# Register loads between the halves of the second product, other scatter slots, other unit periods

## The chip, the core and the metric

The kernel runs on one core of a Trainium2 chip. The metric is the device time of one execution in microseconds; the time of a kernel is the median of its runs. TensorE (PE) multiplies matrices, VectorE (DVE) and ScalarE (ACT) work elementwise, GpSimd (POOL) does elementwise work and issues indirect DMAs, SyncE (SP) issues the other DMAs. Every engine executes its own instructions in program order and waits for the others by semaphores.

## What is computed

A gated linear recurrence over four sequences of 5056 tokens with 256 features, and behind it a mixture of eight experts, of which each token goes to one:

```python
f = lower_bound + (1 - lower_bound) * sigmoid(f_logit)
h = f[:, t] * h + (1 - f[:, t]) * x[:, t]      # for t in range(S); y[:, t] = h
...
logits = y @ w_gate                            # 20224 tokens x 8 experts
e = argmax(logits); gate_w = softmax(logits)[e]
out = gate_w * (relu(y @ w1[e]) @ w2[e])       # w1: 256 x 1024, w2: 1024 x 256
```

## The kernel before

**Front part.** Tokens come in 79 units of 256 (UNIT), with the features on the partitions. For each unit: load (L253), gates on ScalarE and GpSimd (`prep`, L260), the recurrence as a scan on VectorE and the largest magnitude of the result (`scan`, L270), a split into two 16-bit parts (`split`, L290, whose first instruction is the TensorE broadcast L115), and the eight-column router product (`logits`, L315, matmuls L319). After a group of two or four units `route` (L322) picks the expert of each token, and `place` (L343, matmuls L351) counts, for every token, its row in a bucket of its expert. A scatter (L379) then copies 128 token rows into the buckets in HBM: one cast of the row numbers on DVE (L381) and one indirect DMA on POOL (L382). `tile_info` (L397) names the tiles of 128 or 256 tokens that are certain to be full by then; a function `give` (L620) puts them on the list `todo`.

**Expert part.** `fetch` (L500) reads a tile back transposed (SP, L506), with factor and target row (L508), up to three steps ahead. `gemm1` (L513) first loads, for each tile of the step, the offset of its expert's weights into a TensorE register (L515), then makes the first product in four blocks (L526 to L528, three matmuls for the 16-bit parts); a block goes from PSUM through ScalarE (L531) and DVE (L532) into hT. `gemm2` (L552) makes the second product for two halves of 128 tokens, 24 matmuls each (L560 to L562), scales the result (L566) and scatters it to the output by an indirect DMA on POOL (L567). A step takes either two tiles of 128 tokens, in general of two experts, or one of 256. The plan makes all tiles of the first 14 groups 128 tokens long, and those of the later groups 256; a rest of 128-token tiles comes at the end. `step` (L685) runs gemm1 of a new step and then gemm2 of the step before.

**Addresses.** Weight operands have addresses of the form register plus constant. `share_addresses` (L828) rewrites TensorE's stream: it collects up to 16 such sums in a block of register instructions ahead of the matmuls that use them, and starts a new block when 16 are exceeded or a register load comes.

**The order.** After a start written out by hand (ORDER, L44), up to unit 8 and the first step, the loop at L799 interleaves the two parts, in program order, on PE, ACT and DVE. A step has eight slots, and each calls `fill(k)` (L784): k = 0 to 3 after the four blocks of gemm1, 4 in the middle of the first half of gemm2, 5 between the halves, 6 in the middle of the second half, 7 at the end. A unit is planned by `plan_unit` (L776) at a slot number `nxt`: split there, the scan of the next unit two slots later, the gates of the one after it at three, logits at five, the end of a group at ten; `nxt` then moves on by a period of 5 to 8 slots, the longer the more tokens are ready (`ready()`, L673: tokens in `todo` and fetched). Scatters and the `give` behind them wait in the list `held`, and `release` (L628) takes pieces off it: one in slots 0, 2 and 4, one in slots 1 and 3 when more than 6 are held, and two in every slot when fewer than SHORT tokens are ready.

Of the kernel before, what the change touches and what calls it, by code (L numbers as in the profile page):

```python
# [19 lines left out]
E = 8  # L20
F = 1024
NF = F // P
UNIT = 256
GRU = 4
G = 2 * GRU
WE = 2 * 2 * F
# [7 lines left out]
HOWS = ('dve', 'dve', 'dve', 'dve', 'dve', 'dve', 'dve', 'dve', 'dve', 'dve', 'dve', 'dve', 'dve', 'pe', 'pool', 'dve')  # L34
PLO = '000000000011'
DRIP = 1
BACKLOG = 6
MAYBE = 3
LEAD2 = UNIT
LOW = 4 * UNIT  # L40
MID = 5 * UNIT
HIGH = 8 * UNIT
SHORT = 3 * UNIT
ORDER = "Q L X P X T Z L X L A0 P L X X L A1 W T B0 P X L L L P C0 T B1 T F P X Q A2 C1 Q P L A3 B2 L B3 C2 C3 L X T X T L L L F Z X L A4 B4 A6 T P P A5 X T C4 L P B5 B6 C5 C6 F A7 B7 T S Q C7"  # L44
EXPM = 0x7F800000
EVEN = 0x7F000000
# [13 lines left out]
def guaranteed(n, size):  # L60

    return max(0, (n - E * (size - 1)) // size)
# [3 lines left out]
def moe_kernel(ctx: ExitStack, tc: tile.TileContext, x, fl, lb, wg, w1, w2, cst, tok, out, xb, S):  # L66
    nc = tc.nc
# [157 lines left out]
    vals = [(const.tile([P, 3, E], F32, tag=f"val{k}", name=f"val{k}"), {}) for k in range(2)]  # L225
    unit_of, counts = [1], {}
    tk = const.tile([P, NT], I32, tag="tk", name="tk")
    scatters = []

    def free(d, *groups, keep=()):  # L230

        for k in groups:
            tc.declare_no_dep(d.ins, group=k, keep=[s.ins for s in keep], reason="different rows")
# [266 lines left out]
    def fetch(t, tiles):  # L500
        xT = p2.tile([P, 4, UNIT], F16, tag="xT", name=f"xT{t}", bufs=3)
        me = sm.tile([P, 2, 2], F32, tag="me", name=f"me{t}", bufs=5)
        n = 0
        for nt, (off_ap, _, _, skip, nsc) in tiles:
            off = nc.sync.value_load(off_ap, min_val=0, max_val=E * CAP + P - nt)
            d = nc.sync.dma_start_transpose(xT[:, :, n:n + nt], xb16[ds(off, nt), 0:2 * D])  # L506
            guard(d, nsc, skip)
            d = nc.sync.dma_start(me[:, n // P:(n + nt) // P, :], xb[ds(off, nt), D:D + 2].rearrange("(j p) w -> p j w", p=P))  # L508
            guard(d, nsc, skip)
            n += nt  # L510
        return t, tiles, xT, me, n

    def gemm1(t, tiles, xT, me, n, fill):  # L513
        hT = p2.tile([P, 2, NF, UNIT], F16, tag="hT", name=f"hT{t}")
        evs = [nc.tensor.value_load(i[1], min_val=0, max_val=(E - 1) * WE) for _, i in tiles]  # L515
        for b in range(NF // 2):
            ps = pg1.tile([P, 2, UNIT], F32, tag="g1", name=f"g1_{t}_{b}")
            for q in range(2):
                f = 2 * b + q
                a = 0  # L520
                for ev, (nt, _) in zip(evs, tiles):
                    for c in range(2):
                        hi = w1s[:, ds(ev + (c * F + f * P), P)]
                        lo = w1s[:, ds(ev + (2 * F + c * F + f * P), P)]
                        o = ps[:, q, a:a + nt]
                        nc.tensor.matmul(o, lhsT=hi, rhs=xT[:, c, a:a + nt], start=c == 0, stop=False)  # L526
                        nc.tensor.matmul(o, lhsT=hi, rhs=xT[:, 2 + c, a:a + nt], start=False, stop=False)  # L527
                        nc.tensor.matmul(o, lhsT=lo, rhs=xT[:, c, a:a + nt], start=False, stop=c == 1)  # L528
                    a += nt
            hh = hT[:, 0, 2 * b:2 * b + 2, :n]  # L530
            nc.scalar.activation(hh, ps[:, :, :n], AF.Relu)  # L531
            nc.vector.scalar_tensor_tensor(hT[:, 1, 2 * b:2 * b + 2, :n], ps[:, :, :n], 0.0, hh, op0=ALU.max, op1=ALU.subtract)  # L532
            drip(DRIP)
            fill(b)
        return t, n, [ev for ev, (nt, _) in zip(evs, tiles) for _ in range(nt // P)], hT, me, tiles

    def factors(t, n, evs, hT, me, tiles):
        fac = sm.tile([P, 2], F32, tag="fac", name=f"fac{t}", bufs=3)
        ti, a = [], 0
        for nt, (_, _, ei, skip, _) in tiles:  # L540
            j = slice(a // P, (a + nt) // P)
            nc.scalar.activation(fac[:, j], me[:, j, 0], AF.Copy, scale=ei)
            to = me.bitcast(I32)[:, j, 1:2]
            if skip is not None:
                at = sm.tile([P, 1], I32, tag="ti", name=f"ti{t}_{a}", bufs=4)
                nc.vector.tensor_scalar(at, to[:, 0, :], skip, None, op0=ALU.add)
                to = at.unsqueeze(1)
            ti += [to[:, k, :] for k in range(nt // P)]
            a += nt
        return t, evs, hT, fac, ti  # L550

    def gemm2(t, evs, hT, fac, ti, fill):  # L552
        for j, ev in enumerate(evs):
            po = pg2.tile([P, 512], F32, tag="g2", name=f"g2_{t}_{j}")
            for f in range(NF):
                hi = w2s[:, ds(ev + f * D, D)]
                lo = w2s[:, ds(ev + (2 * F + f * D), D)]
                hh = hT[:, 0, f, j * P:(j + 1) * P]
                hl = hT[:, 1, f, j * P:(j + 1) * P]
                nc.tensor.matmul(po[:, :D], lhsT=hh, rhs=hi, start=f == 0, stop=False)  # L560
                nc.tensor.matmul(po[:, :D], lhsT=hh, rhs=lo, start=False, stop=False)  # L561
                nc.tensor.matmul(po[:, :D], lhsT=hl, rhs=hi, start=False, stop=f == NF - 1)  # L562
                if f == NF // 2 - 1:
                    fill(4 + 2 * j)
            ob = p2.tile([P, D], F32, tag="ob", name=f"ob{t}_{j}", bufs=3)
            nc.scalar.activation(ob, po[:, :D], AF.Copy, scale=fac[:, j:j + 1])  # L566
            d = nc.gpsimd.indirect_dma_start(  # L567
                out=out[:, :], out_offset=bass.IndirectOffsetOnAxis(ap=ti[j], axis=0),
                in_=ob, in_offset=None, bounds_check=N - 1, oob_is_err=False)
            free(d, "out")  # L570
            tc.add_to_no_dep_group("out", d.ins)
            fill(5 + 2 * j)
# [3 lines left out]
    while n < NU:  # L576
# [3 lines left out]
        k = guaranteed(n * UNIT - taken, size)  # L580
# [13 lines left out]
    todo, placing, drips, total, held = [], [], [], [], []  # L594
# [33 lines left out]
    def release(n=1):  # L628

        while n and held:  # L630
            held.pop(0)()
            n -= 1

    def drip(n=1):

        for _ in range(n):
            if drips and next(drips[0], True):
                drips.pop(0)
# [32 lines left out]
    queue, fetched, pend, nst = [], [], [], 0  # L671

    def ready():  # L673
        return sum(t for t, _ in todo) + sum(f[4] for f in fetched)

    def prefetch():
        nonlocal nst
        while todo and len(fetched) < 3:
            tiles = [todo.pop(0)]
            if tiles[0][0] == P and todo and todo[0][0] == P:  # L680
                tiles.append(todo.pop(0))
            fetched.append(fetch(nst, tiles))
            nst += 1

    def step(fill, second=True):  # L685

        prefetch()
        if len(pend) > 1:
            gemm2(*factors(*pend.pop(0)), lambda k: None)
        last = factors(*pend.pop(0)) if pend and second else None  # L690
        pend.append(gemm1(*fetched.pop(0), fill))
        prefetch()
        if last:
            gemm2(*last, fill)
        else:
            for k in range(4, 8):
                fill(k)
# [33 lines left out]
    for w in ORDER.split():  # L731
        k, n = w[0], int(w[1:] or 0)
# [43 lines left out]
    def plan_unit(t1, period):  # L776

        nonlocal nxt
        scans1, preps2, split1, logits1 = t1
        coming.extend((nxt + k, a) for k, a in ((0, split1), (2, scans1), (3, preps2), (5, logits1), (10, finish)))  # L780
        coming.sort(key=lambda c: c[0])
        nxt += period

    def fill(k):  # L784
        nonlocal here
        while coming and coming[0][0] <= here:
            coming.pop(0)[1]()
        here += 1
        short = ready() < SHORT
        if short or k in (0, 2, 4) or k in (1, 3) and len(held) > BACKLOG:  # L790
            release(1 + short)

    def flush():
# [5 lines left out]
    while u < NU or coming:  # L799
        r = ready()  # L800
        while u < NU and nxt < here + 8:
            nxt = max(nxt, here)
            plan_unit(tick(u), 5 if r < LOW else 6 if r < MID else 7 if r < HIGH else 8)
            u += 1
        if r >= LEAD2:
            step(fill)
        else:
            flush()
# [6 lines left out]
    while todo or fetched:  # L815
        step(lambda k: None)
# [3 lines left out]
    if spare:  # L820
        n = nc.values_load(total[0])
        last = [fetch(nst + k, tiles) for k, tiles in enumerate((spare[:1], spare[1:]))]
        with tc.If(n > NTAIL - MAYBE):
            for f in last:
                gemm2(*factors(*gemm1(*f, lambda k: None)), lambda k: None)
# [89 lines left out]
```

## Time and profile before

| | |
|---|---|
| median of 3 runs | 1103.1 us (1101.06 to 1103.48) |
| the profiled execution | 1098.53 us, span 1096.8 us |
| mean granted TensorE clock | 0.947 |
| HBM | 58.57 MB read, 43.16 MB written |
| scatters into the buckets, L382 | 158, of 1009 ns each on POOL |
| scatters to the output, L567 | 142 and 20, of 1051 and 971 ns |

In a line of the profile, an engine's busy time is the time in which it has an instruction of its own in work; matmuls overlap, so the 273 ns that one takes at L560 are not the distance between two of them. An idle time in brackets in the timeline is the gap in front of that instruction, with what ended it; "issue" there means that nothing the profile shows was waited for. Register instructions have no rows.

### The profile page before, as it was taken

How to read it: one execution, taken by the hardware profiler on the slowest of the kernel's cores; microseconds unless marked ns; L12 is line 12 of the kernel's file. 1: busy time of each engine (PE TensorE's matmuls, PEld its weight loads, DVE VectorE, ACT ScalarE, POOL GpSimd, SP SyncE). 2: the span in 40 equal slices, each digit the busy share in tenths (PEclk: the TensorE clock that was granted, in tenths of full speed). 3: DMA queues.
4: the chain of work that ended last, by engine and by line, in shares of the span. 5: the costliest groups of instructions: out<-in, count | busy, mean ns of one | idle time of the engine just before them, and what ended most of it. 6: DMA issues, size and time to landing. Idle time of an engine off the chain costs nothing.

```text
span 1096.8 us, 29865 instructions
## 1 busy us (share of the span) xinstructions
PE 956.6 (87%) x10971; PEld 861.8 (79%) x10971; DVE 660.6 (60%) x1827; ACT 497.3 (45%) x971; POOL 509.2 (46%) x517
## 2 busy tenths in 40 slices
PE   3327878988998899998899999999998999999995
PEld 2326777878887788897888888888887888899994
DVE  5789867777656667566677877766655222222321
ACT  4537544545444444454455555545532333333331
POOL 2453765455555455656566665565544112121121
PEclk9557999889999999999999999999999999999998
DMA  7987565776785557656576786677642222222120
GB/s 255 314 274 211 113 134 140 156 145 135 142 157 136 125 133 160 150 137 153 135 177 142 168 175 155 157 142 156 134 104 79 49 50 54 51 53 48 37 49 23
DMA packets 239776, 145.57 MB, mean 133 GB/s; under 512 B 205965, under 2 KB 207247, under 8 KB 237584
## 3 DMA queue, kind: packets, MB, share of 16 engines
q1 hardware_dynamic: 224272, 102.02, 43.8%
q0 software_dynamic: 15360, 41.60, 12.5%
q8 instruction: 93, 1.52, 0.6%
q14 instruction: 51, 0.42, 0.1%
HBM read 58.57 MB, written 43.16 MB: 93 GB/s over the span
## 4 chain that ended last, share of the span: by engine, by line
PE 68%; DVE 14%; issue 8%; ACT 3%; DMA 2%; another core or an unknown queue 2%; POOL 1%; SPq 0%; POOLq 0%; DVEq 0%; ACTq 0%
PE g L528 11%; PE g L526 11%; PE g L527 11%; PE g L560 11%; PE g L562 11%; PE g L561 11%; DVE xt L283 3%; DVE hT L532 2%; DMA ft<-in_f 2%; DVE ft L310 2%; DVE am L286 1%; ACT ft L301 1%; ACT hT L531 1%; PE tp L319 1%
## 5 line engine op out<-in xcount | busy, mean ns | idle before, releaser
L526 PE MATMUL g<-xT,w1s 128*128 128x128 f16 (+1 forms) x1968 | 414.8, 241 | 30.5 <-issue 16.8
L527 PE MATMUL g<-xT,w1s 128*128 128x128 f16 (+1 forms) x1968 | 414.4, 240 | 8.8 <-issue 8.6
L528 PE MATMUL g<-xT,w1s 128*128 128x128 f16 (+1 forms) x1968 | 414.3, 240 | 8.4 <-issue 8.3
L532 DVE SCALAR_TENSOR_TENSOR hT<-g,hT 128x512 f16<-128x512 f32 x324 | 220.2, 687 | 297.1 <-ACT hT L531 256.0
L561 PE MATMUL g<-w2s,hT 128*128 x1296 | 354.2, 273 | 2.6 <-issue 2.6
L560 PE MATMUL g<-w2s,hT 128*128 x1296 | 354.2, 273 | 2.3 <-issue 1.9
L562 PE MATMUL g<-w2s,hT 128*128 x1296 | 354.1, 273 | 0.9 <-issue 0.7
L531 ACT ACTIVATE hT<-g 128x512 f16<-128x512 f32 x324 | 185.6, 591 | 196.0 <-PE g L528 144.2
L382 POOL DMA_INDIRECT buckets<-rows,idx x158 | 159.5, 1009 | 184.7 <-DVE idx L381 120.9
L567 POOL DMA_INDIRECT out_dram<-ob,me x142 | 149.3, 1051 | 194.1 <-ACT ob L566 143.2
L526 PEld LDWEIGHTS <-w1s 128*128 x1968 | 197.1, 100 | 38.0 <-issue 30.0
L527 PEld LDWEIGHTS <-w1s 128*128 x1968 | 197.3, 100 | 24.6 <-issue 17.5
L528 PEld LDWEIGHTS <-w1s 128*128 x1968 | 197.5, 100 | 19.3 <-issue 12.3
L566 ACT ACTIVATE ob<-g,fac 128x256 f32<-128x256 f32 x162 | 76.0, 470 | 179.0 <-PE g L562 161.9
L560 PEld LDWEIGHTS <-hT 128*128 128x128 f16 x1296 | 127.0, 98 | 19.2 <-issue 5.2
L562 PEld LDWEIGHTS <-hT 128*128 128x128 f16 x1296 | 127.1, 98 | 17.8 <-issue 2.8
L561 PEld LDWEIGHTS <-hT 128*128 128x128 f16 x1296 | 127.0, 98 | 15.7 <-issue 1.9
L283 DVE TENSOR_TENSOR_SCAN xt<-ft,xt,xt 128x256 f32<-128x256 f32 (+2 forms) x156 | 113.8, 754 | 5.9 <-POOL xt L268 5.9
L310 DVE SCALAR_TENSOR_TENSOR ft<-xt,m,ft 128x256 f16<-128x256 f32 x154 | 81.2, 546 | 58.2 <-ACT ft L301 44.5
L301 ACT ACTIVATE ft<-xt,m 128x512 f16<-128x512 f32 x79 | 57.0, 721 | 119.1 <-DVE m L298 83.0
L268 POOL TENSOR_TENSOR xt<-gi,xt 128x512 f32<-128x512 f32 x79 | 104.0, 1316 | 5.5
L267 POOL TENSOR_SCALAR gi<-ft 128x512 f32<-128x512 f32 x79 | 57.1, 722 | 78.1 <-ACT ft L265 74.5
(134 smaller groups left out, 755.9 us busy)
## 6 DMA issues: line engine op xcount, KB each, us to landing
ft<-in_f SPq DMA_DIRECT2D x79, 256.0 KB
xt<-in_x SPq DMA_DIRECT2D x79, 256.0 KB
w2s<-in_w SPq DMA_DIRECT2D x14, 1024.0 KB
rows<-ft SPq DMA_TRANSPOSE x158
buckets<-rows,idx POOLq DMA_INDIRECT x158
out_dram<-ob,me POOLq DMA_INDIRECT x142
ws<-in_w SPq DMA_DIRECT2D x2, 1024.0 KB
xT<-buckets SPq DMA_TRANSPOSE x126
```

Of the source, the lines that this page charges most:

```text
L268: nc.gpsimd.tensor_tensor(xt, gi, xt, op=ALU.mult)
L283: nc.vector.tensor_tensor_scan(xt[:, c, a:b], ft[:, c, a:b], xt[:, c, a:b], ini, op0=ALU.mult, op1=ALU.subtract)
L382: d = nc.gpsimd.indirect_dma_start(out=xb[:, :], out_offset=bass.IndirectOffsetOnAxis(ap=idx[:, i:i + 1], axis=0), in_=rows[:, i, 0:ROW], ...
L526: nc.tensor.matmul(o, lhsT=hi, rhs=xT[:, c, a:a + nt], start=c == 0, stop=False)
L527: nc.tensor.matmul(o, lhsT=hi, rhs=xT[:, 2 + c, a:a + nt], start=False, stop=False)
L528: nc.tensor.matmul(o, lhsT=lo, rhs=xT[:, c, a:a + nt], start=False, stop=c == 1)
L531: nc.scalar.activation(hh, ps[:, :, :n], AF.Relu)
L532: nc.vector.scalar_tensor_tensor(hT[:, 1, 2 * b:2 * b + 2, :n], ps[:, :, :n], 0.0, hh, op0=ALU.max, op1=ALU.subtract)
L560: nc.tensor.matmul(po[:, :D], lhsT=hh, rhs=hi, start=f == 0, stop=False)
L561: nc.tensor.matmul(po[:, :D], lhsT=hh, rhs=lo, start=False, stop=False)
L562: nc.tensor.matmul(po[:, :D], lhsT=hl, rhs=hi, start=False, stop=f == NF - 1)
L567: d = nc.gpsimd.indirect_dma_start(out=out[:, :], out_offset=bass.IndirectOffsetOnAxis(ap=ti[j], axis=0), in_=ob, in_offset=None, bounds_c ...
```

## The change

Four constants and the condition for `release` change; the register loads move into a function `bases`, which remembers what it has loaded; and `step` hands gemm2 a `then` that calls `bases` for the next step's tiles in slot 5, before that slot's other work. If no tiles are fetched by then, or the step has no gemm2, gemm1 loads the registers itself as before.

```diff
-BACKLOG = 6
-LOW = 4 * UNIT
+LOW = 3 * UNIT
 MID = 5 * UNIT
-HIGH = 8 * UNIT
-SHORT = 3 * UNIT
+HIGH = 7 * UNIT
+SHORT = 2 * UNIT
...
-    scatters = []
+    scatters, based = [], {}
...
+    def bases(t, tiles):
+
+        if t not in based:
+            based[t] = [nc.tensor.value_load(i[1], min_val=0, max_val=(E - 1) * WE) for _, i in tiles]
+        return based[t]
+
     def gemm1(t, tiles, xT, me, n, fill):
         hT = p2.tile([P, 2, NF, UNIT], F16, tag="hT", name=f"hT{t}")
-        evs = [nc.tensor.value_load(i[1], min_val=0, max_val=(E - 1) * WE) for _, i in tiles]
+        evs = bases(t, tiles)
...
         prefetch()
+
+        def then(k):
+            if k == 5 and fetched:
+                bases(*fetched[0][:2])
+            fill(k)
         if last:
-            gemm2(*last, fill)
+            gemm2(*last, then)
...
         short = ready() < SHORT
-        if short or k in (0, 2, 4) or k in (1, 3) and len(held) > BACKLOG:
+        if short or k in (1, 3) or k == 0 and len(held) > 4 or k == 5 and len(held) > 8:
             release(1 + short)
```

A step with more than LOW, MID and HIGH tokens ready plans its units at periods of 6, 7 and 8 slots, below LOW at 5.

## The prediction

> **What bounds the kernel now.** I read the engines' busy times first, then the stretches, then who TensorE waited for, then single places in the timeline.
>
> ```profile
> span 1096.8 us, 29865 instructions
> PE 956.6 (87%) x10971; PEld 861.8 (79%) x10971; DVE 660.6 (60%) x1827; ACT 497.3 (45%) x971; POOL 509.2 (46%) x517
> ...
> 104.00:300.00 196.00, 167.92 (x2184) 154.92 (x2183) 143.90 (x459) 96.19 (x197) 112.70 (x116) 0.92 0.66 137
> 300.00:560.00 260.00, 233.60 (x3080) 211.38 (x3078) 171.68 (x473) 127.65 (x266) 144.09 (x145) 0.99 0.64 145
> 560.00:800.00 240.00, 233.87 (x2339) 208.47 (x2337) 172.73 (x481) 128.37 (x258) 145.18 (x148) 1.00 0.70 154
> 800.00:850.00 50.00, 45.31 (x405) 38.23 (x403) 27.17 (x111) 14.40 (x31) 21.90 (x22) 0.97 0.37 91
> 850.00:1050.00 200.00, 200.00 (x2198) 183.56 (x2196) 54.26 (x91) 68.15 (x140) 36.91 (x38) 1.00 0.23 50
> ```
>
> The columns of a stretch are its length, then busy time (and instructions) of PE, PEld, DVE, ACT, POOL, then granted clock, DMA share and GB/s. The reader is to see that TensorE is the bound wherever expert products run: from 850 us on it has no gap at all, and no change to planning can shorten that part. What can be won lies in its gaps: 28.1 us in 104 to 300, 26.4 in 300 to 560 (steps of two 128-token tiles up to here), 6.1 in 560 to 800 (steps of one 256-token tile), 4.7 in 800 to 850. The first 104 us, before the planned loop, are not touched. The clock adds to it: a mean grant of 0.92 over 196 us, if it switches between full and half, is 16% or 31 us at half, so about 16 us of work lost, and another 3 us in the next stretch; those are estimates from this column.
>
> ```profile
> PE g L526 <- issue: 16.2, 20, 2.1
> PE g L528 <- issue: 7.4, 15, 1.1
> PE g L527 <- issue: 7.4, 16, 1.0
> PE tp L115 <- DVE am L286: 5.5, 3, 2.1
> PE g L526 <- DVE hT L532: 4.1, 3, 3.2
> PE tp L115 <- DVE idx L381: 4.0, 3, 2.4
> PE g L526 <- DMA xT<-buckets: 2.5, 1, 2.5
> ```
>
> These are TensorE's waits between 104 and 560 us: total, times, longest. The largest releaser is "issue", which means that no semaphore held the instruction: TensorE's own instruction stream was late. Where the long ones sit shows in the timeline:
>
> ```profile
> 143.49 0.23 PE L526 MATMUL g<-xT,w1s 128*128 128x128 f16 x1 [1.87 <-issue]
> ...
> 232.11 0.23 PE L115 MATMUL tp<-half,am 128*128 128x128 bf16 x1 [2.38 <-DVE idx L381]
> 234.41 0.28 PE L526 MATMUL g<-xT,w1s 128*128 128x128 f16 x1 [2.07 <-issue]
> ...
> 261.41 0.23 PE L526 MATMUL g<-xT,w1s 128*128 128x128 f16 x1 [0.39 <-PE tp L319]
> ...
> 274.48 0.23 PE L526 MATMUL g<-xT,w1s 128*128 128x128 f16 x1 [1.58 <-issue]
> ...
> 381.92 0.23 PE L526 MATMUL g<-xT,w1s 128*128 128x128 f16 x1 [1.54 <-issue]
> ...
> 483.04 0.23 PE L526 MATMUL g<-xT,w1s 128*128 128x128 f16 x1 [0.46 <-PE tp L319]
> ...
> 495.42 0.23 PE L115 MATMUL tp<-half,am 128*128 128x128 bf16 x1 [1.34 <-DVE am L286]
> 497.24 0.23 PE L526 MATMUL g<-xT,w1s 128*128 128x128 f16 x1 [1.60 <-issue]
> ...
> 523.56 0.23 PE L526 MATMUL g<-xT,w1s 128*128 128x128 f16 x1 [1.60 <-issue]
> ```
>
> Each L526 here is the first of a step, right behind work that the planner put into slot 7 (end of the second product). There L515 loads the expert offsets into TensorE registers. Where the instruction ahead, L115, had to wait, the stream could not get past it, and the load follows in the open. Six boundaries are of this kind: 1.87, 2.07, 1.58, 1.54, 1.60 and 1.60, together 10.3 us. How much of one is the load?
>
> ```profile
> 420.87 0.23 PE L115 MATMUL tp<-half,am 128*128 128x128 bf16 x1 [0.47 <-issue]
> 421.26 0.23 PE L526 MATMUL g<-xT,w1s 128*128 128x128 f16 x1 [0.16 <-issue]
> 421.32 0.22 PE L527 MATMUL g<-xT,w1s 128*128 128x128 f16 x1
> ...
> 705.09 0.27 PE L562 MATMUL g<-w2s,hT 128*128 x1
> 705.20 0.22 PE L115 MATMUL tp<-half,am 128*128 128x128 bf16 x1
> 705.25 0.27 PE L526 MATMUL g<-xT,w1s 128*128 128x256 f16 x1
> ```
>
> At 420.87 L115 stands in slot 0, inside the first product: behind it comes a fresh block of address arithmetic (16 addresses and their two products, made by share_addresses) but no load, and L526 starts 0.39 us later. At 495.42 it takes 1.82 us. So two loads cost 1.82 - 0.39 = 1.43 us when nothing covers them, the arithmetic 0.34 (0.39 less the 0.05 from L115 to L526 at 705.20). At 705.20 the stream was ahead and the whole thing costs nothing.
>
> **The change part by part.** I walked the planner's counters (units, slots, held pieces) through lines 774 to 808 with the old and the new constants; with the old ones they put L115 at the step boundaries at which the trace has it.
>
> *Register loads.* They leave the boundary and go to slot 5, ahead of that slot's other work, between 24 matmuls of the first half and 24 of the second. **Slot 7:** the old schedule has 9 steps of two tiles with TensorE work in it; the six above and two smaller ones (0.39 and 0.46, behind L319) pay, 11.1 us together. What stays is the arithmetic, 0.16 to 0.34 each. The new periods put work there in 13 such steps; at the old share of 8 in 9 and 0.25 each that is 2.9. Term: -8.2 us. **Slot 6:** work there leaves 12 matmuls, 1.3 us at the 0.11 us between starts at 705, to cover 1.77 us.
>
> ```profile
> 313.01 0.23 PE L526 MATMUL g<-xT,w1s 128*128 128x128 f16 x1 [0.21 <-PE g L562]
> ...
> 510.07 0.23 PE L526 MATMUL g<-xT,w1s 128*128 128x128 f16 x1 [0.64 <-PE g L562]
> ```
>
> Seven boundaries show such a rest, these the smallest and the largest, 2.8 us in all, out of 14 steps of two tiles with work in slot 6. With the load at slot 5 the place with the same 12 matmuls of cover is slot 4; the new schedule has work there in 11 such steps: 11 x 2.8/14 = 2.2. Term: -0.6. Where the last wait lies a slot earlier (24 matmuls, 2.6 us of cover) old boundaries show nothing, so slot 3 is taken at nothing. In steps of one 256-token tile both halves shared one block of arithmetic; the load between them makes a second one necessary: 39 x 0.34 = 13 us if uncovered, nothing behind 24 matmuls; I take nothing, since the boundary at 705 hides as much and a load. No new semaphore is waited on: the offsets were already read by SP when the tile was fetched. If one were, everything of TensorE's stream would queue behind it.
>
> The Trainium skill, "Runtime: NRT & Kernel Launch", section "Instruction fetch mechanics", prices a register load at about 200 ns; this trace's two at 1.43 us disagree, and the measured value decides. By the page the slot-7 term would be only about 8 x 0.4 = 3.2 us, an estimate, and the sum some 5 us smaller.
>
> *Clock.* Fewer idle microseconds ahead of a stretch mean fewer returns to half clock. About 9 of 54.5 idle us from 104 to 560 go, a sixth; a sixth of the 19 lost is 3. Ends 0 and 6; I take -2, below the proportion because small gaps may not trip it.
>
> *Periods.* A shorter ready queue now suffices for the next period (3 units for 6 slots, 7 for 8). Counted out: fives go from 15 to 12, sixes 17 to 31, sevens 31 to 17, eights 7 to 10. They sum to 450 and 445 slots, so production ends a step earlier, not later: pieces held longer do not count as ready, which pulls the period back. The gain is more distance from a scan (slot +2) to the L115 of the next unit:
>
> ```profile
> 193.40 0.29 PE L115 MATMUL tp<-half,am 128*128 128x128 bf16 x1 [2.14 <-DVE am L286]
> ```
>
> This one follows a period of 5; the 9.5 us in the two L115 rows above fall on fives, sixes and sevens alike. Ends -4 and +4; I take -1.
>
> *Scatters.* Three of eight slots become two, with two more under backlog: L381 (0.14 us on DVE) and L382 (1.0 us on POOL) number the same 158 as before, and by the counters nearly all planned ones now fall into slots 0, 1 and 3. POOL has room:
>
> ```profile
> L382 POOL DMA_INDIRECT buckets<-rows,idx x158 | 159.5, 1009 | 184.7 <-DVE idx L381 120.9
> ...
> L381 DVE CAST idx<-mx 128x1 int32<-128x1 f32 x142 | 18.2, 142 | 0.0
> ```
>
> The queue loses the slot-4 scatters ahead of the first L567 and gets them behind the last one of the step before. I take nothing; ends -3 and +3, about 20 casts times 0.14 either way. If POOL's slack were gone, the late thing would be L268 and with it the scan.
>
> Sum: -8.2 - 0.6 - 2 - 1 = -11.8. The profiled execution took 1098.53 us (span 1096.8 plus 1.7 around it) and becomes 1086.7; it lies 4.6 below the median 1103.1 of the three runs, on which I put the same gain: about **1091 us**.
>
> **The rivals.** (a) *The stall moves to the middle and is paid in every step: slower.* At a boundary the stream has had 48 long matmuls to run ahead, at slot 5 only 24, after a first product whose 128-column matmuls start 0.06 us apart (421.26 and 421.32) and leave it little lead. Price: the part of 1.77 us that the lead doesn't cover, over 32 steps of two tiles. It decides from 0.37 us a step (32 x 0.37 = 11.8); at 0.6 us, what slot 6 cost at its worst, it is +19 - 12 = +7, so 1110. For it: the seven rests above show that lead runs short after 12 matmuls. Against: after 24 none shows. Chance 0.15.
>
> (b) *Work arrives too late.* On average 4.1 pieces are held, not 2.3, and the queue stands at two steps' worth or less at the start of 8 of the 32 steps of two tiles, 3 before.
>
> ```profile
> 159.16 0.22 PE L526 MATMUL g<-xT,w1s 128*128 128x128 f16 x1 [2.55 <-DMA xT<-buckets]
> POOL rows L375 <- DMA buckets<-rows,idx: 18.8, 9, 2.9
> ```
>
> The first row is the one place where TensorE waited for tokens, at the old low point of one step; the second shows POOL already waiting for rows buffers, and by the counters the tightest of these (the third buffer's reuse after units 18 and 19) shrinks from 5 slots of slack to 1. At 2.55 us for four of the five further such steps this takes 10 back: 1101, within the noise of no change. Against: two steps' worth is still 20 us of lead. Chance 0.13.
>
> (c) *The gaps only change owner.* With registers early, the boundary waits for DVE instead; the "issue" rows shrink, the L115 and L532 rows grow by half as much, and what is left is 5 us: 1098. Chance 0.10.
>
> (d) *More than forecast.* With TensorE's stream full at each boundary the short issue gaps inside L526 to L528, 31.0 us in the three rows above less the 11.1 of the boundaries, shrink too, by a half: -10 more, 1081. For it: they come in steps of two tiles, where the lead is smallest. Chance 0.20.
>
> **How the numbers follow.** Forecast 0.42, (a) 0.15, (b) 0.13, (c) 0.10, (d) 0.20. A measurement of this kernel tells about 0.2%, 2.2 us, from no change. Forecast, (d) and most of (c) are faster: 0.42 + 0.20 + 0.08 = 0.70. Same: most of (b) and the rest of (c), 0.08 + 0.02 = 0.10, and 0.03 from the weak end of (a): 0.13. Slower: the rest of (a) and of (b), 0.17. The range takes the unknown ends of clock, periods and scatters: -11.8 - 4 - 4 - 3 gives 1080, which holds most of (d), and upward it takes (c) and (b) up to 1105, leaving most of (a) out.
>
> **What would show it.** In the changed profile the first L526 behind an L115 should idle under 0.4 us, "issue" before L526 between 104 and 560 fall from 16.2 to about 7, the clock of 104 to 300 rise above 0.92. Rests of 0.2 to 0.6 before L560 in the middle of a step only where slot 4 has work. Wrong would be: L560 idling 0.4 us or more in most steps of two tiles (a), more waits for xT or longer rows-buffer waits (b), or L115 and L532 rows growing while issue falls (c).

## The result, and the profile after

The changed kernel takes 1072.7 us (median of 4 runs, 1068.6 to 1075.4) against 1102.1 for the kernel before: ratio 0.9731, 95% interval 0.9697 to 0.9765. It is faster, as forecast, but by 29 us where the forecast was 12, and lies below the range of 1080 to 1105. The profiled execution took 1071.38 us (span 1069.7) where that of before took 1098.53.

One thing has to be known to read the later numbers: the same kernel before gives 1096 to 1102 us in two of the six sessions on chips and 1044 to 1046 us in the other four, steadily within each, so every ratio below is against runs of before in its own session, and I call the first kind gappy (for a reason that will show) and the second kind quiet. A ratio is the record's, with its 95% interval in brackets, and can differ by up to 0.3% from the quotient of the two medians beside it.

The page's head and the stretches of the changed kernel, with the columns as before (length, busy time of PE, PEld, DVE, ACT, POOL, clock, DMA share, GB/s):

```profile
span 1069.7 us, 29977 instructions
PE 949.1 (89%) x10971; PEld 858.1 (80%) x10971; DVE 652.1 (61%) x1827; ACT 498.1 (47%) x971; POOL 505.5 (47%) x517
...
104.00:300.00 196.00, 169.40 (x2223) 154.35 (x2222) 144.74 (x460) 99.03 (x202) 109.68 (x113) 0.94 0.61 136
300.00:560.00 260.00, 244.56 (x3256) 224.86 (x3254) 182.80 (x538) 140.57 (x293) 160.61 (x165) 1.00 0.77 162
560.00:800.00 240.00, 238.75 (x2381) 213.90 (x2380) 172.43 (x513) 122.66 (x246) 143.39 (x147) 1.00 0.69 149
800.00:850.00 50.00, 46.35 (x396) 39.96 (x396) 14.40 (x26) 14.54 (x29) 11.38 (x12) 0.93 0.25 59
850.00:1050.00 200.00, 200.00 (x2304) 184.83 (x2302) 54.98 (x96) 68.49 (x142) 37.07 (x38) 1.00 0.20 48
```

TensorE's idle time went from 26.4 to 15.4 us in 300 to 560 and from 6.1 to 1.3 in 560 to 800; in 104 to 300 it stayed near 27. More matmuls stand in the same stretch (3256 for 3080), so the program ends sooner. Its waits between 104 and 560 us (total, times, longest; lines moved: L531 to L533 are the first product, L565 begins the second, L114 is the old L115):

```profile
PE tp L114 <- DVE am L285: 10.5, 7, 2.9
PE g L533 <- issue: 6.1, 12, 1.2
PE g L531 <- issue: 5.6, 14, 1.2
PE g L532 <- issue: 4.0, 10, 0.5
PE g L531 <- DVE hT L537: 3.8, 3, 3.2
PE tp L114 <- DVE idx L380: 3.3, 1, 3.3
PE g L565 <- DVE am L285: 2.2, 1, 2.2
```

Issue ahead of the first product fell from 31.0 to 15.7 us; the waits of L114 for DVE rose from 9.5 to 13.8; and there is a new row, L565 behind DVE. The step boundary itself, in the timeline, at two places where slot 7 holds an L114:

```profile
220.16 0.29 PE L114 MATMUL tp<-half,am 128*128 128x128 bf16 x1 [3.25 <-DVE idx L380]
220.55 0.29 PE L531 MATMUL g<-xT,w1s 128*128 128x128 f16 x1
...
384.89 0.22 PE L114 MATMUL tp<-half,am 128*128 128x128 bf16 x1
384.95 0.22 PE L531 MATMUL g<-xT,w1s 128*128 128x128 f16 x1
```

Behind a blocked L114 the first product now follows after 0.39 us, where it took 1.8; behind one that wasn't blocked it follows after 0.06.

To divide the gain I took, over 104 to 850 us, each distance between successive matmul starts, less the 0.109 us that a 256-column matmul and the 0.056 us that a 128-column one takes when nothing is late, and summed what is left over 0.03 us by what stands behind it:

| TensorE time lost ahead of | before | after | change |
|---|---|---|---|
| a matmul of the first product, behind other work (mostly step boundaries) | 22.3 | 4.9 | -17.4 |
| a matmul of the first product, behind another of it | 51.6 | 34.8 | -16.8 |
| a matmul of the second product | 11.1 | 14.0 | +2.9 |
| L115, L319, L351 (they wait for DVE and ACT) | 13.1 | 18.0 | +4.9 |
| sum | 98.1 | 71.7 | -26.4 |

What a row holds depends by up to 2 us on what the narrower matmuls are allowed; the sum is nearly all of the 27.1 us between the two spans. About half of what was won, 16.8 of 34.2 us, is inside the first product, where the change edits nothing. Some 9 us of these 16.8 are gaps that the profile puts down to issue (29 to 20 us), 4 are matmuls that start some 0.05 us late each while the clock stands at half, and 3.6 are waits for other engines (8.1 to 4.5).

### The profile page after: what moved, and what is told of

It reads as the page before. It is cut to its first block, busy times and chain, and to the rows that moved or that the text cites. A ratio compares the mean times of both kernels' runs of the same rounds, so it can differ in the third digit from the quotient of the medians.

```text
span 1069.7 us, 29977 instructions
## 1 busy us (share of the span) xinstructions
PE 949.1 (89%) x10971; PEld 858.1 (80%) x10971; DVE 652.1 (61%) x1827; ACT 498.1 (47%) x971; POOL 505.5 (47%) x517
## 4 chain that ended last, share of the span: by engine, by line
PE 74%; DVE 12%; issue 5%; DMA 3%; ACT 2%; POOL 1%; another core or an unknown queue 1%; SPq 0%; POOLq 0%; DVEq 0%; ACTq 0%
PE g L531 12%; PE g L533 12%; PE g L532 12%; PE g L565 12%; PE g L567 12%; PE g L566 12%; DVE xt L282 2%; DVE ft L309 2%; DVE hT L537 2%; PE tp L318 1%; DMA ft<-in_f 1%; DVE w2s L210 1%; DVE am L285 1%; DMA w2s<-in_w 1%
## 5 line engine op out<-in xcount | busy, mean ns | idle before, releaser
L531 PE MATMUL g<-xT,w1s 128*128 128x128 f16 (+1 forms) x1968 | 409.4, 239 | 10.9 <-issue 5.6
L533 PE MATMUL g<-xT,w1s 128*128 128x128 f16 (+1 forms) x1968 | 409.1, 239 | 6.7 <-issue 6.7
L532 PE MATMUL g<-xT,w1s 128*128 128x128 f16 (+1 forms) x1968 | 409.2, 239 | 4.1 <-issue 4.1
L565 PE MATMUL g<-w2s,hT 128*128 x1296 | 354.3, 273 | 4.3 <-DVE am L285 2.2
L567 PE MATMUL g<-w2s,hT 128*128 x1296 | 354.4, 273 | 2.2 <-issue 2.2
L566 PE MATMUL g<-w2s,hT 128*128 x1296 | 354.3, 273 | 1.7 <-issue 1.7
L381 POOL DMA_INDIRECT buckets<-rows,idx x158 | 162.8, 1030 | 176.7 <-DVE idx L380 99.3
L572 POOL DMA_INDIRECT out_dram<-ob,me x142 | 145.7, 1026 | 177.5 <-ACT ob L571 120.1
L531 PEld LDWEIGHTS <-w1s 128*128 x1968 | 195.3, 99 | 19.2 <-issue 10.5
L533 PEld LDWEIGHTS <-w1s 128*128 x1968 | 195.4, 99 | 13.7 <-issue 6.2
L566 PEld LDWEIGHTS <-hT 128*128 128x128 f16 x1296 | 127.1, 98 | 18.9 <-issue 4.7
L565 PEld LDWEIGHTS <-hT 128*128 128x128 f16 x1296 | 127.1, 98 | 18.4 <-issue 4.2
L567 PEld LDWEIGHTS <-hT 128*128 128x128 f16 x1296 | 127.2, 98 | 17.5 <-issue 2.4
L282 DVE TENSOR_TENSOR_SCAN xt<-ft,xt,xt 128x256 f32<-128x256 f32 (+2 forms) x156 | 116.1, 764 | 5.9 <-POOL xt L267 5.9
L309 DVE SCALAR_TENSOR_TENSOR ft<-xt,m,ft 128x256 f16<-128x256 f32 x154 | 78.4, 530 | 57.9 <-ACT ft L300 44.2
```

Of the source, the lines that this page charges most:

```text
L282: nc.vector.tensor_tensor_scan(xt[:, c, a:b], ft[:, c, a:b], xt[:, c, a:b], ini, op0=ALU.mult, op1=ALU.subtract)
L381: d = nc.gpsimd.indirect_dma_start(out=xb[:, :], out_offset=bass.IndirectOffsetOnAxis(ap=idx[:, i:i + 1], axis=0), in_=rows[:, i, 0:ROW], ...
L572: d = nc.gpsimd.indirect_dma_start(out=out[:, :], out_offset=bass.IndirectOffsetOnAxis(ap=ti[j], axis=0), in_=ob, in_offset=None, bounds_c ...
```

## The experiments

**Where the change is undone in parts.** Four kernels, run together in a quiet session. e1_load is the kernel before with the moved loads alone:

```diff
+    def bases(t, tiles):
...
-        evs = [nc.tensor.value_load(i[1], min_val=0, max_val=(E - 1) * WE) for _, i in tiles]
+        evs = bases(t, tiles)
...
+            if k == 5 and fetched:
+                bases(*fetched[0][:2])
```

> Only the register loads move to slot 5; periods, SHORT and the release condition are those of before. Theory L (the loads hold most of the gain, because the fuller instruction stream also removes short issue gaps inside the first product): 1079 to 1087 us, ratio 0.979 to 0.986, issue ahead of the first-product matmuls between 104 and 560 us from 31 to under 18 us. Theory S (periods and scatters hold most of it, the loads only the step boundaries as in the forecast): 1091 to 1096, ratio 0.990 to 0.994, issue from 31 to some 20.

Measured: 1039.2 against 1044.2 us, ratio 0.9952 (0.9934 to 0.9969). Three later runs of the same edit, all in quiet sessions, gave 0.9934 (0.9909 to 0.9959), 0.9914 (0.9887 to 0.9941) and 0.9915 (0.9894 to 0.9937). Neither theory's time applies, as the base is another; the ratio lies on the side of theory S.

e2_periods changes LOW and HIGH alone:

```diff
-LOW = 4 * UNIT
+LOW = 3 * UNIT
-HIGH = 8 * UNIT
+HIGH = 7 * UNIT
```

> Only LOW and HIGH change (3 and 7 units). Theory L: within 4 us of before, ratio 0.996 to 1.003. Theory S: 8 us or more faster, ratio under 0.993, with fewer and shorter waits of L115 for the scan's maximum.

Measured: 1036.4 us, 0.9933 (0.9918 to 0.9949). The periods are worth as much as the loads, more than the -1 us of the forecast.

e3_scatter changes SHORT and the release condition alone:

```diff
-SHORT = 3 * UNIT
+SHORT = 2 * UNIT
-        if short or k in (0, 2, 4) or k in (1, 3) and len(held) > BACKLOG:
+        if short or k in (1, 3) or k == 0 and len(held) > 4 or k == 5 and len(held) > 8:
```

> Only SHORT (2 units) and the release condition change. Theory L: within 4 us of before, ratio 0.996 to 1.004. Theory S: 8 us or more faster, ratio under 0.993.

Measured: 1048.3 us, 1.0044 (1.0028 to 1.0060): it costs.

e4_noload has both of these edits, and the loads where they were:

> The changed kernel with the register loads back at the start of gemm1: periods, SHORT and release condition changed. Theory L: 1094 to 1102 us, ratio 0.993 to 1.0, since the new schedule puts work into slot 7 of 13 steps of two tiles instead of 9 and each exposes the load. Theory S: 1078 to 1088, ratio 0.978 to 0.987.

Measured: 1045.5 us, 1.0012 (0.9993 to 1.0031); the same kernel later, in quiet sessions again, 0.9986 (0.9969 to 1.0004) and 1.0009 (0.9988 to 1.0031). The new schedule without the loads gains nothing there.

**The two ends beside each other.** r0_before and r1_after are the two kernels unaltered, in a gappy session:

> The kernel before, unaltered, for a profile on the chip that runs the others. The first experiments' chip gave it 1044 us, not 1102, so the profile should differ from the first one in some kind of gap. If the chip feeds TensorE's instruction stream faster, the issue gaps inside the first product (31 us between 104 and 560 us with the boundaries) should be nearly gone and the six boundaries of slot 7 still there; if its transfers are faster, the waits for DMA should have shrunk instead.

Measured: 1093.1 against 1096.5 us, 0.9985 (0.9953 to 1.0017). What sets the sessions apart shows in the waits of TensorE from 104 to 850 us. First this kernel in the gappy session:

```profile
PE g L526 <- issue: 16.9, 27, 1.9
PE g L527 <- issue: 9.6, 16, 1.1
...
PE g L528 <- issue: 5.9, 13, 1.0
```

Then e12_noload (the schedule of the change, loads at the start of gemm1) in a quiet one, since the kernel before has no profile from a quiet session; e12 takes the same time as before there (0.9986). L527 and L528 have no issue row among its longest:

```profile
PE tp L115 <- DVE am L286: 11.8, 8, 4.0
PE g L526 <- issue: 5.8, 8, 1.7
PE tp L115 <- DVE idx L381: 5.6, 2, 4.0
PE g L526 <- DVE hT L532: 2.3, 3, 1.7
```

In the quiet session the boundary's issue is left, and the short issue gaps inside the products are gone; the stretch from 800 to 850 us shows it for the second product:

```profile
800.00:850.00 50.00, 44.70 (x400) 38.23 (x398) 23.23 (x92) 14.39 (x31) 20.26 (x21) 0.97 0.34 83
```

```profile
800.00:850.00 50.00, 50.00 (x461) 44.81 (x459) 12.86 (x19) 17.00 (x34) 9.80 (x10) 1.00 0.24 54
```

The first is r0_before, the second e12_noload. By the count of the table TensorE loses some 94 us between 104 and 850 us in r0_before and 48 in e12_noload, which is most of the 49 us between their times. These gaps are not scattered by chance: counted in matmuls, 27 of the 45 of over 0.2 us inside the first product in the first profile have one in r0_before within three matmuls; with the positions of one profile shifted by an arbitrary amount about one would. The start of one string of them, in the first profile and in r0_before (the whole string spans numbers 3099 to 3114 and 3100 to 3111 of the 10971 matmuls):

```profile
342.79 0.22 PE L528 MATMUL g<-xT,w1s 128*128 128x128 f16 x1 [0.45 <-issue]
343.56 0.22 PE L527 MATMUL g<-xT,w1s 128*128 128x128 f16 x1 [0.33 <-issue]
344.28 0.22 PE L528 MATMUL g<-xT,w1s 128*128 128x128 f16 x1 [0.51 <-issue]
```

```profile
340.86 0.22 PE L526 MATMUL g<-xT,w1s 128*128 128x128 f16 x1 [0.44 <-issue]
341.60 0.22 PE L527 MATMUL g<-xT,w1s 128*128 128x128 f16 x1 [0.36 <-issue]
342.34 0.23 PE L526 MATMUL g<-xT,w1s 128*128 128x128 f16 x1 [0.47 <-issue]
```

Each gap is some 0.4 us, one every 0.74 us, and nothing that the profile shows stands behind it. The queue that carries the instructions moved the same in both kinds of session: 93 packets, 1.52 MB and 0.6% of the DMA engines' time in r0_before and in e12_noload.

> The changed kernel, unaltered, beside the kernel before on one chip. If the 27 us of the first measurement came mostly from short issue gaps that this chip doesn't have (theory F: a fuller stream rides them out), the gain shrinks to what boundaries and waits give: 4 to 14 us on 1044, ratio 0.987 to 0.996. If it is the loads and periods by themselves (theory L or S), it stays at 22 us or more, ratio 0.979 or less.

Measured in the gappy session: 1067.9 against 1096.5 us, 0.9764 (0.9727 to 0.9801). Issue ahead of the first product from 104 to 850 us, 32.4 us in r0_before, is 8.4 here:

```profile
PE g L531 <- issue: 3.1, 10, 0.7
...
PE g L532 <- issue: 3.1, 8, 0.5
...
PE g L533 <- issue: 2.2, 7, 0.5
```

The condition named in the expectation, a chip without the gaps, wasn't met there. It was met in a later, quiet session, with the same kernel as r2_after:

> The changed kernel again, as the yardstick of the three above. On a chip with before at 1095 to 1103: ratio 0.971 to 0.981 as in both comparisons so far. On a chip with before at 1044: 0.984 to 0.996, since half of the 27 us gained were issue gaps that the first experiments' chip hardly shows.

Measured: 1040.5 against 1046.0 us, 0.9955 (0.9940 to 0.9971). So the gain is 29 us in both gappy sessions and 5 us in a quiet one. That is the consequence that theory F named; its mechanism, that a fuller stream rides the gaps out, is not shown by this.

**Ahead of the blocking instruction, but without the matmuls behind it.** e5_slot7 loads in slot 7 instead of 5, with the old schedule:

```diff
-            if k == 5 and fetched:
+            if k == 7 and fetched:
```

> As e1_load (old periods and release condition), but the loads of the next step stand in slot 7, at the end of the second product and ahead of that slot's L115, L319 or L351, so that no second block of arithmetic is needed. If what matters is that the load stands ahead of the instruction that blocks the stream, this does as well as e1_load, 1034 to 1041 us. If the 24 matmuls behind it are needed as cover, it lies between e1_load and before, 1041 to 1046.

Measured in the gappy session: 1090.1 us, 0.9946 (0.9921 to 0.9971). Against r0_before the loss ahead of the first product at boundaries falls from 19.0 to 9.5 us between 104 and 560 (same count as in the table), but that inside the first product goes from 42.4 to 46.5. The boundary gaps and the inner gaps are two things: getting the load ahead of the blocked L115 mends the first, not the second.

**The price of a load, and the cover.** e6_double is the kernel before with each load made twice:

```diff
         evs = [nc.tensor.value_load(i[1], min_val=0, max_val=(E - 1) * WE) for _, i in tiles]
+        evs = [nc.tensor.value_load(i[1], min_val=0, max_val=(E - 1) * WE) for _, i in tiles]
```

> The kernel before with every register load of gemm1 made twice. At 0.7 us a load (the price read from the first profile) the six boundaries of slot 7 and those of slot 6 pay 1.4 us more each, and part of the others: 12 to 30 us slower, 1056 to 1074. At 0.2 us a load, 2 to 6 us slower, 1046 to 1050.

Measured in the gappy session: 1136.6 us, 1.0388 (1.0346 to 1.0430), 40 us slower, above the expectation. Its waits from 104 to 850 us; L527 is the first matmul of the first product here:

```profile
PE g L527 <- issue: 48.3, 38, 3.3
...
PE g L529 <- issue: 3.4, 7, 0.8
...
PE g L528 <- issue: 1.2, 4, 0.4
```

The loss at the 31 boundaries of steps of two tiles, with what stands in front of them, is 60.4 us against 18.7 in r0_before: 41.7/31 = 1.35 us for two loads, nearly the 1.43 read from the first profile. It is paid in steps of two tiles throughout (30 of the 31 first matmuls start over 1.2 us late), not only behind a blocked instruction: one set of loads was all that the stream's lead at a boundary covers. In steps of one 256-token tile, with one load to double, it is less (some 6 us over the 26 from 560 to 850 us). The rows of L528 and L529 show something that was not looked for. They are the second and third line of the first product, and issue ahead of them is 4.6 us, where r0_before in the same session has 15.5 (9.6 and 5.9 at L527 and L528): the short gaps inside the first product shrink here too, although the product starts later, with the stream behind and not ahead.

e15_double5 doubles the loads at slot 5, in the kernel with the moved loads alone (e13_load, run beside it):

> Loads at slot 5, all else as before. With before at 1095 to 1103 us: theory F (a fuller stream alone rides out the issue gaps) 0.976 to 0.985; theory J (it needs the new schedule too) 0.988 to 0.996. With before at 1044 to 1046: 0.991 to 0.996.

> As e13, with every load made twice at slot 5. If 24 matmuls there cover one set of loads with little to spare, the second set (1.43 us in steps of two tiles) shows in most of them: 20 to 45 us slower than e13, as at the start of gemm1. If slot 5 has cover to spare, up to 8 us slower.

Measured: 1037.0 us for e13 (0.9915, above) and 1078.0 for e15, which is 1.0312 (1.0288 to 1.0336) of before and 41 us more than e13. L567 begins the second product here, L573 scales its result:

```profile
PE g L567 <- issue: 9.9, 14, 1.8
PE g L567 <- ACT ob L573: 9.6, 8, 1.3
```

In nearly all of the 31 steps of two tiles up to 560 us there is a loss ahead of the second half, 43.9 us in all against 4.4 in e13_load, 39.5/31 = 1.27 us a step. Slot 5 covers one set of loads and hardly more, like the boundary.

**Which parts go together.** In the quiet session of r2_after, the loads again and with one more part each:

> The same kernel as e1_load (loads at slot 5, all else as before), now beside the changed kernel on one chip. On a chip that gives before some 1095 to 1103 us: theory L (loads alone hold most) ratio 0.976 to 0.985; theory J (the parts only pay together, since the new schedule without the loads gained nothing) ratio 0.988 to 0.996. On a chip that gives before 1044: 0.995 again.

Measured: 0.9934, given with e1 above.

> Loads at slot 5 and the new LOW and HIGH; SHORT and release condition of before. On a chip with before at 1095 to 1103: theory L within 0.4% of e7_load; theory J at least 0.6% below e7_load, and near the changed kernel if the periods are the partner of the loads. On a chip with before at 1044 the two parts add up if they are independent: 0.995 x 0.993 = 0.988.

Measured: 1031.6 against 1046.0 us, 0.9862 (0.9842 to 0.9882); again in a later session 0.9874 (0.9853 to 0.9896). Loads and periods add up, and this kernel beats the changed one (0.9955) in the same session.

> Loads at slot 5, new SHORT and release condition; LOW and HIGH of before. Alone the scatter part cost 0.4% on the 1044 us chip. Theory L: within 0.4% of e7_load. Theory J: near the changed kernel if the scatters are the partner of the loads, otherwise 0.2 to 0.6% above e7_load.

Measured: 1046.3 us, 1.0007 (0.9993 to 1.0022). The scatter edit takes back all that the loads give. The counters of the planner suggest why: pieces that are held longer don't count as ready, so more units are planned at the shortest period, and the scan of a unit stands closer to the L115 that needs it. For the quiet runs, units planned at 5 slots and L115's waits for DVE from 104 to 850 us:

| kernel | units at 5 slots | L115 waits for DVE, us |
|---|---|---|
| e3_scatter, e9_load_scatter | 24 | 21.5, 21.1 |
| e1_load, e7_load, e10_load, e13_load | 15 | 16.1, 16.0, 13.3, 16.3 |
| e4_noload, e12_noload, e14_noload, r2_after | 12 | 17.4, 17.4, 18.0, 14.4 |
| e2_periods, e8_load_periods, e11_load_periods | 5 | 10.4, 6.3, 5.5 |

The two ends stand apart; between 12 and 15 units the waits show no order.

The rows of the two ends, e3_scatter and e11_load_periods (the same edits as e8):

```profile
PE tp L115 <- DVE am L286: 19.6, 13, 2.2
...
PE tp L115 <- DVE idx L381: 1.9, 1, 1.9
```

```profile
PE g L566 <- DVE am L286: 7.5, 1, 7.5
PE tp L115 <- DVE am L286: 4.5, 3, 2.1
...
PE tp L115 <- DVE idx L381: 1.0, 1, 1.0
```

The 7.5 us row in the second fence is one wait ahead of the second half of a second product (L566 begins it here), and the same stands in r2_after with 7.4 us:

```profile
151.00 0.13 DVE L436 SCALAR_TENSOR_TENSOR ii<-inf,cs 128x8 int32<-128x8 f32 x1
...
152.93 0.37 PE L565 MATMUL g<-w2s,hT 128*128 x1 [7.37 <-DVE am L285]
```

It falls into the one step that starts with a single step's work ready. Its next tiles were named only then: L436, the counterpart of L437, writes their offsets at 151.00, and the load in slot 5 waits for it with the second half of the product behind it. That L436 and not the L285 named is what ended it I read from the order of the two streams. The time fits: L436 ends at 151.13, and 1.77 us for two loads and their arithmetic lead to 152.90. But L285 follows L436 at a fixed distance, so the fit does not tell the two apart, and no run took the wait away.

**Not settled.** Four more kernels were meant for a gappy session, to tell which part makes the larger gain there; the sessions were quiet, and they repeat what is told above.

> Loads at slot 5, all else as before. In a session with before at 1095 to 1103 us: if a fuller instruction stream alone rides out the short issue gaps (theory F) 0.976 to 0.985; if the lead at slot 5 is used up by gaps as well and the gain needs the new schedule (theory J) 0.988 to 0.996. In a session with before at 1044 to 1046: 0.993 to 0.996 as twice so far.

> Loads at slot 5 and the new LOW and HIGH, scatters of before. With before at 1095 to 1103: theory F within 1% below e10; theory J 0.970 to 0.980, at or below the changed kernel. With before at 1044 to 1046: 0.986 again.

> New periods, SHORT and release condition, loads at the start of gemm1. With before at 1095 to 1103: theory F 0.995 to 1.005; if the new schedule itself avoids the issue gaps, 0.975 to 0.988. With before at 1044 to 1046: 1.00 as before.

> New periods, SHORT and release condition, loads at the start of gemm1. With before at 1095 to 1103: theory F 0.995 to 1.005; if the new schedule itself avoids the issue gaps, 0.975 to 0.988. With before at 1044 to 1046: 0.998 to 1.002.

Measured: e10 1036.0 us (0.9914), e11 1031.9 (0.9874), e12 1044.2 (0.9986), against 1045.9; e14 1045.7 (1.0009) against 1045.1.

## Why the prediction was right and wrong

**Slots 7 and 6** (terms -8.2 and -0.6): right. In the span for which they were worked out, 104 to 560 us, the loss ahead of the first product behind other work fell by 13.4 us and that ahead of the second product rose by 4.8, together -8.6. Of the 13.4, 1.8 are the wait for tokens (2.5 to 0.7), and of the 4.8, 2.2 are the wait for offsets told below; what is left, 11.6 won at the boundary and 2.6 paid in the middle, is near the 11.0 (8.2 and 2.8) and the 2.2 of the sum. The mechanism stood as described: the boundary keeps 0.39 us of arithmetic. The price of 1.43 us for two loads was confirmed by both doubled kernels (1.35 and 1.27 us a step). The Trainium skill's "Runtime: NRT & Kernel Launch", section "Instruction fetch mechanics", gives about 200 ns a load; these loads, which read from SBUF, cost some 0.65 us each, and the measured value decides.

**"No new semaphore is waited on"**: wrong in one step. At the low point of the queue the load stands in front of 24 matmuls and waits for offsets that DVE hasn't written: 2.2 us in the profile after, 7.4 in r2_after.

**Rival (a)**, the stall in the middle of every step: it didn't come, but the margin was thin. With one set of loads e13_load loses 4.4 us ahead of the second halves over all steps of two tiles; with a second set e15 loses 43.9.

**Rivals (b) and (c)**: the wait for xT did not grow (2.5 to 0.7 us), and (b) came only as the wait for offsets above. Of (c) a part came: the waits of L115 for DVE grew by 4.3 us while issue shrank by 15.3.

**Periods** (-1) and **scatters** (nothing): each was wrong in size, and they oppose each other. In quiet sessions the periods gain 0.7%, some 7 us, and the scatter edit costs 0.4% alone and 0.7 to 0.9% beside the loads. The prediction counted the fives of the whole change, 15 to 12, and so saw only the sum; counted for each edit alone they are 5 and 24. In the profile after the waits of L114 for DVE rose in place of falling. No run has either edit by itself in a gappy session.

**Clock** (-2): the grant went from 0.92 to 0.94 in 104 to 300 us, from 0.99 to 1.00 in 300 to 560 and from 0.97 to 0.93 in 800 to 850; 0.02 x 196 + 0.01 x 260 - 0.04 x 50 is an estimated 4.5 us of full-rate work, more than forecast and within the bounds given.

**The step that failed** is the one that left the short issue gaps inside L526 to L528 out of the sum. The prediction saw them, 20 us of rows, and made them rival (d) with a half of them going, -10 us, at 0.20. Inside the first product the gaps put down to issue went by 9 us in the first pair of profiles (29 to 20) and by 19 us from r0_before to r1_after (30 to 11). That is the largest part of the difference between -12 and -27. The rest is spread: the clock, shorter waits for other engines inside the first product, and some 4 us at the boundaries behind 560 us, mostly waits for DVE, for which the sum has nothing.

That the gaps are a thing of the session, and no property of the kernel alone, is shown by the two kinds of sessions: without them the same change gains 5 us, so the forecast of 12 holds in neither kind. What in the change makes them shrink is open. Rival (d) gave a fuller stream at the start of the first product as the reason. e5_slot7, where the load stays next to the first product and the inner gaps stay too, fits it. e6_double speaks against it: there the product starts later, and the inner gaps shrink as well. Neither the loads at slot 5 without the new schedule nor the new schedule without the loads fell into a gappy session, and why these sessions have the gaps is open as well.

## What to carry to other kernels

A register load at the head of a TensorE stage cost some 0.65 us here, as much as six matmuls of 256 columns, and was free only while the stream was ahead; put it where long matmuls follow and before, not behind, an instruction that may wait, and check the steps in which its own source is late. When a change has parts, count what each does to the schedule alone: two edits of a planner can cancel, and here the version without the scatter edit is the best in quiet sessions, 0.986 to 0.987 against 0.9955. And run the kernel before in every session: its own time moved by 5% between them, more than the change.

## What the runs showed of the hardware that was not expected

The same program took 1096 to 1102 us in two sessions and 1044 to 1046 in four, with no difference in the granted clock that would carry it (0.954 in r0_before, 0.950 in e1_load) and with the same DMA bytes. It is not a matter of the chip either: what the record numbers as chip 10 gave a gappy session, and half an hour later a quiet one. The difference lies in gaps of some 0.4 us in TensorE's own stream, mostly at the same places of the program, in the gappy sessions only. And a second set of two register loads cost 1.3 us in each step of two tiles, at either place, where the first set had cost 0.14 us a step between the halves (4.4/31) and at most 0.60 at the boundary (18.7/31, other waits included).
